# A three-stage kernel on one core: the fade of the sub-chunk attention moves from the values to the queries

## Chip, core and metric

The kernel runs on one core of a Trainium2 chip. The metric is the device time of one execution in microseconds (us); the median of several executions counts. TensorE multiplies matrices, VectorE, ScalarE and GpSimd work on elements, and the DMA queues of SyncE (SP) and ScalarE move data between HBM and the on-chip memories SBUF and PSUM.

## What is computed

Three stages run one after the other: a retention attention over 4 x 8 heads of 768 positions with 64 values each, and two MLPs over the 3072 tokens (512 to 2048 to 512), one with x cos(x), one with a quadratic ramp. The change touches the attention only.

```python
def _attn_ref(q, k, v):
    B, H, S, D = q.shape
    gamma = 1.0 - 2.0 ** (-5.0 - np.arange(H, dtype=np.float32))
    scale = 1.0 / np.sqrt(D)
    state = np.zeros((B, H, D, D), dtype=np.float32)
    for t in range(S):
        state = gamma[None, :, None, None] * state + np.einsum('bhd,bhe->bhde', k[:, :, t], v[:, :, t])
        y[:, :, t] = scale * np.einsum('bhd,bhde->bhe', q[:, :, t], state)
```

The power of gamma that a query at position t carries is called its fade here; the powers that the keys carry are their decay.

## The kernel before

**Order.** The instruction order of every engine is written out by hand. The work is a list of steps. Step i issues the first product of the first MLP for one block of 512 tokens and 128 hidden features (`first`, L681, 12 matmuls), the activation of it (`act`), and the second product of the step three before it (`second`, L768, 12 matmuls). The attention, which makes the blocks of tokens, and the conversion of weights are woven into the first 40 steps. Step 5 begins at 62.2 us in the trace, step 10 at 90.4, step 11 at 95.8, step 12 at 102.4, step 13 at 111.6, step 16 at 137.4.

**The attention.** There are 24 chunks n: six places in the sequence of 128 positions, for each of four batches. Chunks 0 to 7 work on whole chunks, chunks 8 to 23 (n >= NEW) on sub-chunks of 64. For those, `scores64` (L487 for the scores, L498 for the new state) runs on TensorE in step 11, 12, 13, 14 for chunks 8 to 11 and in every second step from 16 for the rest. `masks64` on VectorE then multiplies the scores by the table `mtab` into the tile m (L523, two instructions) and adds the state into w (L536, two or four). One step later `attend` multiplies w by m on TensorE (L580). The tile m holds queries in the two halves where row block and half agree, and masked scores in the other two. `finish_high` multiplies the result by the table `dtab` on VectorE (L614), ScalarE copies the high part (L139), and `finish_low` subtracts it on VectorE (L622). `decay_k` multiplies the keys by a table on GpSimd (L448); `decay_q` does the same to the queries of chunks 4 to 7 alone (L458). In a step of n >= NEW the scores of chunks 8 to 11 stand behind `second`, those of the later chunks ahead of it.

**The conversions.** Weights come as 64-bit numbers and are converted in a chain of steps: a load to `raw` on SP (L189), two VectorE instructions one step later (L203, L206), a third with its ScalarE partner and a GpSimd add (L221, L213, L230), and in the third step a ScalarE copy and GpSimd subtraction (L139, L142) for weights that stay, or a store on ScalarE's queue (L239). A new conversion begins in steps 5 to 11, 16 to 27, and then in odd steps and from step 34.

**The tables.** `mtab` and `dtab` have one buffer each. `load_dtab` is issued on SP in steps 8, 16, 24 and 32 for the next place in the sequence. SP's queue works in order, so a load that waits for its buffer holds those behind it.

Of the kernel before, what the change touches and what calls it, by code (L numbers as in the profile page):

```python
# [17 lines left out]
ALU = mybir.AluOpType  # L18
# [22 lines left out]
def tile_retention_mlp_mlp(  # L41
# [16 lines left out]
    nc = tc.nc  # L58
    NCH = qk.shape[0]
    T, DM = out.shape  # L60
    NF = w1.shape[0]
    NH = NF // 2
    NP = DM // P
    NC = kdec.shape[1]
    NB = T // TB
    D = 64
    CB = TB // C
    NEW = 2 * CB
# [49 lines left out]
    def duo(x, y):  # L118
        if min(x, y) < 6:
            return bank(x), bank(y)  # L120
        t = both()
        return t[:, x - 6, :], t[:, y - 6, :]

    def single(x):
        return bank(x) if x < 6 else both()[:, x - 6, :]
# [12 lines left out]
    def high_part(hi, x):  # L138
        nc.scalar.activation(out=hi, in_=x, func=AF.Copy)  # L139
# [200 lines left out]
    class Attention:  # L340
# [111 lines left out]
            )  # L452

        def decay_q(self, n):
            if n >= NEW:
                return
            self.qd[n] = self.ring("kq", 3 * TB // 2, 2)[:, :TB].rearrange("p (c t) -> p c t", c=NP)
            nc.gpsimd.tensor_tensor(out=self.qd[n], in0=self.t[n][:, 0], in1=self.qdec, op=ALU.mult)  # L458
# [149 lines left out]
        def finish_high(self, n):  # L608
            j, o = divmod(n, CB)
            if o == 0:  # L610
                xt[0, j] = [xpool.tile([P, NP, TB], F32R, tag=t, name=t) for t in ("xh", "xl")]
            if n >= NEW:
                y = self.y[n]
                nc.vector.tensor_tensor(  # L614
                    out=y, in0=y, in1=self.dtab.rearrange("p (c t) -> p c t", c=NP), op=ALU.mult
                )
            high_part(xt[0, j][0][:, :, o * C:(o + 1) * C], self.y[n])

        def finish_low(self, n):
# [25 lines left out]
    def send_x():  # L645
        for d, t in pieces[:2]:
            nc.scalar.dma_start(out=d, in_=t)
        del pieces[:2]
# [23 lines left out]
    def first(k, b, j, hbank):  # L672
        (wh, wl), (xh, xl) = wt[0, j, 0], xt[k, b]
        h = bank(hbank)
        terms = [(c, w, x) for c in range(NP) for w, x in ((wh, xh), (wl, xh))]
        terms += [(c, wh, xl) for c in range(NP)]
        if (k, b, j) == (0, 0, 1):

            terms.sort(key=lambda t: t[1] is wl)
        for i, (c, w, x) in enumerate(terms):  # L680
            nc.tensor.matmul(  # L681
                out=h, lhsT=w[:, c * P:(c + 1) * P], rhs=x[:, c, :],
                start=(i == 0), stop=(i == len(terms) - 1),
            )
        hs[k, b, j] = h

    def act(k, b, j, done=(), fill=(), mid=(), end=()):


        done = iter(done)  # L690
        now = Parts(k, b, j)
        now.rounded()
        last = parts.pop() if parts else None
        if last:
            last.high()
        now.fraction()
        if last:
            last.low()
        evacuate(done, 2)
        for f in mid:  # L700
            f()
        now.cosine()
        evacuate(done, 2)
        for f in fill:
            f()
        conv.advance()
        for f in end:
            f()
        parts.append(now)
# [592 lines left out]
    def run():  # L1302
        i = 0
        with ExitStack() as es:
            att = Attention(es)
# [6 lines left out]
            todo = [Convert(0, j, a, True) for _, _, j, a in order]  # L1312
# [5 lines left out]
            y = dict(enumerate([c for c in todo[:10] if c.a == 1], 1))  # L1318
            x = dict(enumerate(x))
            todo = todo[10:]  # L1320
# [140 lines left out]
            for n in range(CB, NCH):  # L1461
                c = n % CB
                if n < 3 * CB:
                    i = 11 * (n // CB - 1) + c
# [3 lines left out]
                else:  # L1468
                    i = NH * (n // CB - 1) + 2 * c
# [7 lines left out]
            place = {1: (2, 3), 2: (1, 0)}  # L1477
            for i in range(NH * (NB - 1)):
                load_t, load_kq, load_v, decay, early, late, attend = plan[i]
                now = 5 <= i < 12 if i < 2 * NH else (i < 3 * NH + 4 or i % 2 or i > 33) and bool(todo)  # L1480
                conv.start(todo.pop(0) if now else None, stage)
                first(*steps[i], 4 + i % 2)
                for n in load_t:
                    att.load_t(n)
                    att.load_w(n)
                for n in load_kq:
                    att.load_kq(n)
                for n in load_v:
                    att.load_v(n)
                    att.load_k(n)  # L1490
                if i % NH == NH - 1:
                    att.load_mtab((i + 9) // NH)
                elif i % NH == 0 and i:
                    att.load_dtab((i + 8) // NH)
                for n in decay if i >= LAG else ():
                    att.decay_q(n)
                    att.decay_k(n)
                mid, end, fill = [], [], []
                for n in attend:
                    by, bk = place.get(i, (7, 6))  # L1500
                    yb, kb = duo(by, bk)
                    att.attend(n, yb)
                    att.kv(n, kb)
                    mid += [lambda n=n: att.finish(n), lambda n=n: att.update(n)]
                for n in early:
                    att.scores(n, (6, 7))
                    mid.append(lambda n=n: att.masks(n))
                done = second(i - LAG) if i >= LAG else ()
                for m, b in (((0, 0),), ((1, 0),), ((2, 2), (3, 3)))[i] if i < LAG else ():
                    att.kv(m, single(b))  # L1510
                for n in late:
                    att.scores(n, (6, 7))
                    end.append(lambda n=n: att.masks(n))
                if i < LAG:
                    opening(i, CB + i - 1)
                    for c in {0: [x[2]], 1: [y[2]], 2: [y[3], y[4]]}[i]:
                        c.load(stage)
                    if i < 2:
                        att.load_t(CB + 2 + i)
                else:  # L1520
                    if i - 1 in y:
                        c = y[i - 1]
                        if i == LAG:
                            mid += [c.one, c.two]
                            fill += [c.three, c.four, c.five, c.six]
                        else:
                            for f in (c.one, c.two, c.three, c.four):
                                f()
                            mid += [c.five, c.six]
                    act(*steps[i], done, fill, mid, end)  # L1530
                    if i == LAG:
                        y[5].load(stage)
                send_x()
                if i in (3, 6):
                    store_parts(i // 6)
                elif i >= 2 * NH and i % NH == 2:
                    store_parts(steps[i][1])
# [7 lines left out]
        with ExitStack() as es:  # L1545
            stage = es.enter_context(tc.tile_pool(name="stage1", bufs=1, reuse_waits="tile"))
            todo = [Convert(*mja, False, True, store=True) for mja in order2[FIRST:READY]]
# [3 lines left out]
            while i < len(steps):  # L1551
# [3 lines left out]
                now = l < NH - 1 if k == 0 else l != NH - 1 and (l != 3 or b > 2) or len(todo) > len(order2) - READY  # L1555
# [5 lines left out]
                n = blocks.index((k, b)) + 1  # L1561
# [40 lines left out]
def _tables(H, S, D):  # L1602

    g = _GAMMA(H).reshape(H // 2, 2)
    scale = 1.0 / math.sqrt(D)
    s, t = np.arange(C)[:, None], np.arange(C)[None, :]
    low = np.where(s <= t, t - s, 0)
    mask = np.where(s <= t, scale, 0.0)[None, None] * g.T[:, :, None, None] ** low
    mask = mask.transpose(2, 0, 1, 3).reshape(C, -1)
    tt = np.arange(C, S)  # L1610
    qd = scale * g[:, :, None] ** (tt - REF)
    qd = qd.reshape(H // 2, 2, -1, C).transpose(2, 1, 0, 3)
    qd = np.repeat(qd, D, axis=1).reshape(-1, 2 * D, H // 2 * C)
    ss = np.arange(S).reshape(-1, C)
    kd = g.reshape(-1)[None, None, :] ** -(ss.T[:, :, None] - REF).astype(np.float64)

    gh = g.T.reshape(2, 2, 2).transpose(0, 2, 1)[::-1]
    tabs = []
    for j in range(2, S // C):
        at = j * C + np.arange(C).reshape(2, D) - REF  # L1620
        grow = gh[:, None, :, :, None, None] ** -at.T[None, :, None, None, :, None].astype(np.float64)
        grow = grow * (np.arange(D)[:, None] <= np.arange(D))[None, :, None, None, None, :]
        fade = scale * g.T[:, :, None, None] ** at.astype(np.float64)
        fade = np.broadcast_to(fade[:, None], (2, D, H // 2, 2, D))
        tabs.append([a.reshape(2 * D, -1) for a in (grow, fade)])
    return [np.ascontiguousarray(a, dtype=np.float32) for a in (mask, qd[0], kd, np.array(tabs))]
# [60 lines left out]
```

## Time and profile before

| | |
|---|---|
| median of 3 runs | 1109.35 us |
| lowest, highest | 1104.76, 1109.6 us |
| profiled execution: its own time | 1102.34 us |
| its span, first to last instruction | 1100.5 us |
| mean granted TensorE clock | 0.996 |
| busy: TensorE | 1071.2 us (97%) |
| busy: VectorE | 802.5 us (73%) |
| busy: GpSimd | 614.9 us (56%) |
| busy: ScalarE | 603.3 us (55%) |

An engine's busy share is a mean over stages with different limits. A view by stretches says where TensorE, the busiest engine, still has idle time; the chain of work that ended last says what it waited for there. A line number names an instruction of the kernel (L614 is line 614); PE is TensorE, DVE is VectorE, ACT is ScalarE, POOL is GpSimd.

### The profile page before, as it was taken

The numbers are of one execution on the slowest core, as the hardware profiler recorded it, in microseconds if no ns is written. First come the engines' busy times: TensorE is split into PE (matmuls) and PEld (weight loads), VectorE is DVE, ScalarE is ACT, GpSimd is POOL, SyncE is SP. The second block draws the span as 40 slices with busy tenths as digits, with TensorE's granted clock in tenths as the row PEclk, the third lists the DMA queues.
The fourth block names the chain that finished last, engine by engine and source line by source line (L and its number), as shares of the span: only waits on it lengthen the run. The fifth ranks groups of instructions, "written<-read, shape, count | busy, mean of one in ns | idle before, by whom it ended". The sixth has DMA issues, their size and how long they took to land.

```text
span 1100.5 us, 17904 instructions
## 1 busy us (share of the span) xinstructions
PE 1071.2 (97%) x6286; PEld 867.0 (79%) x6286; DVE 802.5 (73%) x1101; ACT 603.3 (55%) x1078; POOL 614.9 (56%) x525
## 2 busy tenths in 40 slices
PE   8999999999999999999999899999999999999996
PEld 5677788878888888878887788788888778888884
DVE  5778878887667446859763477777887777978776
ACT  3444334333355445545562666777577676666663
POOL 3734212221246367878995457786559785554642
PEclk9999999999999999999999999999999999999998
DMA  9498389896667589998978576989588899576542
GB/s 341 171 290 277 107 242 308 270 307 186 212 207 267 193 275 324 335 327 283 313 256 284 198 250 224 316 270 385 200 264 288 293 313 366 173 244 205 180 145 86
DMA packets 139896, 279.94 MB, mean 254 GB/s; under 512 B 15520, under 2 KB 41760, under 8 KB 139808
## 3 DMA queue, kind: packets, MB, share of 16 engines
q1 hardware_dynamic: 128000, 257.31, 71.1%
q10 hardware_dynamic: 11808, 21.50, 5.5%
q8 instruction: 50, 0.82, 0.3%
q14 instruction: 38, 0.31, 0.1%
HBM read 195.39 MB, written 83.36 MB: 253 GB/s over the span
## 4 chain that ended last, share of the span: by engine, by line
PE 78%; DMA 9%; DVE 5%; ACT 2%; POOL 2%; issue 2%; SPq 1%; ACTq 0%; DVEq 0%; POOLq 0%
PE b L768 20%; PE b L681 20%; PE b L951 17%; PE y L967 16%; PE b L580 2%; DMA wo<-wp 1%; DMA xTl<-xl 1%; PE b L487 1%; DVE big L1033 1%; DMA qk<-in_qk 1%; DMA xb2t20h<-xhi 1%; DMA xb1t20h<-xhi 1%; PE b L498 1%; DMA wp<-whi 1%; DMA xh<-xTh 1%
## 5 line engine op out<-in xcount | busy, mean ns | idle before, releaser
L719 ACT ACTIVATE r<-b 128x512 int32<-128x512 f32 x96 | 57.1, 595 | 193.1 <-PE b L681 149.9
L724 DVE SCALAR_TENSOR_TENSOR r<-b,r 128x512 f32<-128x512 f32 x96 | 66.1, 688 | 120.1 <-ACT r L719 118.3
L230 POOL TENSOR_TENSOR cf<-cf,cs 128x512 int32<-128x512 int32 x42 | 54.3, 1293 | 145.0 <-DVE cf L221 109.7
L1025 DVE TENSOR_TENSOR xh<-y,xh 128x1024 f32<-128x1024 f32 x88 | 107.0, 1220 | 26.1 <-PE y L967 24.9
L768 PE MATMUL b<-gh,wo 128*128 128x512 f32 x384 | 98.4, 390 | 2.0 <-DVE o L779 1.7
L1103 POOL TENSOR_TENSOR ft<-r,f 128x512 f32<-128x512 f32 x24 | 31.1, 1296 | 121.0 <-PE y L967 91.7
L681 PE MATMUL b<-xh,wi 128*128 128x512 f32 x384 | 95.4, 390 | 0.9 <-DMA xh<-xTh 0.9
L967 PE MATMUL y<-wi,wo 128*128 128x512 f32 x360 | 92.3, 391 | 3.3 <-POOL wi L992 1.8
L951 PE MATMUL b<-wih,wi 128*128 128x512 f32 x320 | 87.4, 390 | 2.8 <-ACT wih L139 2.4
L1025 DVE TENSOR_TENSOR xl<-y,xl 128x1024 f32<-128x1024 f32 x64 | 77.9, 1217 | 12.9 <-PE y L967 12.9
L967 PE MATMUL y<-gh,wo 128*128 128x512 f32 x272 | 85.1, 394 | 2.3 <-DVE xh L1025 2.3
L768 PEld LDWEIGHTS b<-gh,wo 128*128 128x128 f32 x384 | 71.8, 188 | 17.9 <-DVE o L779 2.4
L681 PEld LDWEIGHTS b<-xh,wi 128*128 128x128 f32 x384 | 71.9, 188 | 16.6 <-DMA xh<-xTh 1.8
L967 PEld LDWEIGHTS y<-wi,wo 128*128 128x128 f32 x360 | 67.1, 188 | 19.4 <-POOL wi L992 3.1
L737 ACT ACTIVATE gh<-b 128x512 fp32r<-128x512 f32 x96 | 57.1, 594 | 39.3 <-DVE b L733 39.0
L681 PE MATMUL b<-xh,wih 128*128 128x512 f32 x192 | 75.8, 397 | 2.2 <-ACT wih L139 0.9
L768 PE MATMUL b<-gh,woh 128*128 128x512 f32 x192 | 77.4, 408 | 0.5 <-ACT woh L139 0.5
L681 PE MATMUL b<-xh,wil 128*128 128x512 f32 x192 | 74.4, 390 | 0.0
L768 PE MATMUL b<-gh,wol 128*128 128x512 f32 x192 | 74.0, 391 | 0.0
L951 PEld LDWEIGHTS b<-wih,wi 128*128 128x128 f32 x320 | 59.8, 188 | 16.4 <-ACT wih L139 2.8
L992 POOL TENSOR_TENSOR gl<-ft,gh 128x512 fp32r<-128x512 f32 x56 | 71.8, 1301 | 1.3 <-ACT gh L139 1.3
L733 DVE TENSOR_TENSOR b<-b,r 128x512 f32<-128x512 f32 x96 | 66.6, 694 | 2.5 <-ACT r L730 0.3
(168 smaller groups left out, 2769.7 us busy)
## 6 DMA issues: line engine op xcount, KB each, us to landing
wi<-wp SPq DMA_DIRECT2D x66, 512.0 KB, 4.8
wo<-wp SPq DMA_DIRECT2D x66, 512.0 KB, 5.1
raw<-in_w SPq DMA_DIRECT2D x64, 512.0 KB, 6.1
wp<-whi SPq DMA_DIRECT2D x48, 256.0 KB, 3.2
wp<-s SPq DMA_DIRECT2D x32, 256.0 KB, 3.2
w<-cf ACTq DMA_DIRECT2D x26, 256.0 KB, 5.4
xTh<-xh ACTq DMA_DIRECT2D x24, 256.0 KB, 5.7
xTl<-xl ACTq DMA_DIRECT2D x24, 256.0 KB, 6.2
```

Source lines behind the costliest of these rows:

```text
L230: nc.gpsimd.tensor_tensor(out=f, in0=f, in1=self.s, op=ALU.add)
L681: nc.tensor.matmul(out=h, lhsT=w[:, c * P:(c + 1) * P], rhs=x[:, c, :], start=(i == 0), stop=(i == len(terms) - 1),)
L719: nc.scalar.activation(out=self.r.bitcast(I32), in_=self.h, func=AF.Identity, scale=INV_2PI, bias=0.25)
L724: nc.vector.scalar_tensor_tensor(out=self.r, in0=self.h, scalar=INV_2PI, in1=self.r.bitcast(I32), op0=ALU.mult, op1=ALU.subtract,)
L733: nc.vector.tensor_tensor(out=self.h, in0=self.h, in1=self.r, op=ALU.mult)
L737: nc.scalar.activation(out=self.gh, in_=self.h, func=AF.Copy)
L768: nc.tensor.matmul(out=acc[k, b][e], lhsT=w[:, s], rhs=g, start=(begin and i == 0), stop=(last and i == 2),)
L951: nc.tensor.matmul(out=to, lhsT=w[:, c * P:(c + 1) * P], rhs=x, start=begin and n == 0, stop=n == len(terms) - 1, skip_group_check=not begin,)
L967: nc.tensor.matmul(out=to[:, e, :], lhsT=w[:, e * P:(e + 1) * P], rhs=a, start=begin and m == 0, stop=m == 2, skip_group_check=not begin,)
L992: eng.tensor_tensor(out=lo, in0=self.f.pop((g, q)), in1=hi.bitcast(F32), op=ALU.subtract)
L1025: nc.vector.tensor_tensor(out=a, in0=y, in1=a, op=ALU.add)
L1103: nc.gpsimd.tensor_tensor(out=o, in0=x, in1=z, op=ALU.subtract)
```

## The change

The fade of chunks 8 to 23 is no longer applied to the result of the attention. `decay_q` now multiplies the queries in m by `dtab` on GpSimd, in place, in two instructions per chunk, one for each half of the partitions. That covers the products of the query with the state and the scores of those halves where the query comes from m. The other scores use a query that is loaded apart; their fade is multiplied into the table `mtab` when it is made. `load_dtab` for the next place is issued after the fade of the last chunk of a place, in the step of that fade, and no longer every eight steps. Conversions begin in steps 5 to 10 instead of 5 to 11, and in steps 16 to 28 instead of 16 to 27.

```diff
         def decay_q(self, n):
+            if n >= NCH:
+                return
             if n >= NEW:
+                for r in range(2):
+                    h = slice(r * D, (r + 1) * D)
+                    q = self.m[n][h, r].rearrange("p c u t -> p (c u t)")
+                    nc.gpsimd.tensor_tensor(out=q, in0=q, in1=self.dtab[h], op=ALU.mult)
                 return
...
-            if n >= NEW:
-                y = self.y[n]
-                nc.vector.tensor_tensor(
-                    out=y, in0=y, in1=self.dtab.rearrange("p (c t) -> p c t", c=NP), op=ALU.mult
-                )
             high_part(xt[0, j][0][:, :, o * C:(o + 1) * C], self.y[n])
...
-                now = 5 <= i < 12 if i < 2 * NH else (i < 3 * NH + 4 or i % 2 or i > 33) and bool(todo)
+                now = 5 <= i < 11 if i < 2 * NH else (i < 3 * NH + 5 or i % 2 or i > 33) and bool(todo)
...
-                elif i % NH == 0 and i:
-                    att.load_dtab((i + 8) // NH)
+                elif i == NH:
+                    att.load_dtab(2)
                 for n in decay if i >= LAG else ():
                     att.decay_q(n)
                     att.decay_k(n)
+                    if n > NEW and n % CB == CB - 1:
+                        att.load_dtab(n // CB + 1)
...
+        most = fade.reshape(2, 2, 2, 2, D).transpose(0, 2, 1, 3, 4)
+        most = np.where(np.eye(2)[:, :, None, None, None] > 0, 1.0, most)
+        grow = grow * most[::-1, None]
```

## Rows read from the trace of the kernel before

**Rows 1.** Busy time by stretch: stretch, length, PE, PEld, DVE, ACT, POOL; clock; DMA.

```profile
84.60:102.40 17.80, 17.78 (x137) 14.57 (x137) 14.64 (x21) 9.67 (x18) 10.98 (x9) 1.00 0.91 309
102.40:144.40 42.00, 38.58 (x505) 30.32 (x506) 34.46 (x58) 13.65 (x24) 9.99 (x9) 1.00 0.46 137
144.40:300.00 155.60, 155.60 (x1577) 125.00 (x1577) 120.97 (x215) 59.73 (x105) 34.52 (x29) 1.00 0.83 256
```

**Rows 2.** Chain that ended last, 84 to 146 us: start, length, what.

```profile
101.27 0.62 PE b L487 x32
...
102.36 2.96 PE b L681 x12
105.33 1.08 issue
106.41 1.15 PE b L580 x32
...
114.60 1.46 issue
...
124.25 0.40 issue
```

**Rows 3.** VectorE in order of time, 96 to 113 us: start, length, instruction, idle before.

```profile
96.16 1.15 DVE L203 TENSOR_SCALAR cf<-raw 128x512 f32<-128x512 f32 x1 [1.09 <-DMA raw<-in_w]
...
97.69 0.68 DVE L221 SCALAR_TENSOR_TENSOR cf<-raw,cf 128x512 int32<-128x512 int32 x1
...
99.22 0.69 DVE L724 SCALAR_TENSOR_TENSOR r<-b,r 128x512 f32<-128x512 f32 x1 [0.24 <-ACT r L719]
...
100.43 0.61 DVE L203 TENSOR_SCALAR cf<-raw 128x512 f32<-128x512 f32 x1
...
101.41 1.78 DVE L221 SCALAR_TENSOR_TENSOR cf<-raw,cf 128x512 int32<-128x512 int32 x1
103.11 1.38 DVE L523 TENSOR_TENSOR qk<-b,mtab 64x512 f32<-64x512 f32 x2
104.53 1.78 DVE L536 TENSOR_TENSOR w<-b,w 64x256 f32<-64x256 f32 x4
...
108.31 0.69 DVE L614 TENSOR_TENSOR b<-b,dtab 128x512 f32<-128x512 f32 x1
109.66 0.69 DVE L622 TENSOR_TENSOR xl<-b,xh 128x512 fp32r<-128x512 f32 x1 [0.66 <-ACT xh L139]
...
111.07 1.77 DVE L221 SCALAR_TENSOR_TENSOR cf<-raw,cf 128x512 int32<-128x512 int32 x1
```

**Rows 4.** Lines L458 and L448: duration ns min/median/max, first and last start, forms.

```profile
L458 POOL TENSOR_TENSOR kq<-qk,w x4: 1273/1299/1472, 25.8 to 49.5; 128x512 f32<-128x512 f32 x4
...
L448 POOL TENSOR_TENSOR kd<-kd,kdec_sb x21: 1037/1046/1500, 28.3 to 282.9; 128x512 f32<-128x512 f32 x17, 64x512 f32<-64x512 f32 x4
```

**Rows 5.** Tile dtab, 80 to 110 us: its load on SP, and issue to landing.

```profile
L375 SPq DMA_DIRECT2D dtab<-in_tabs x1: 585/585/585, 89.1 to 89.1; - x1
...
DMA to landing us min/median/max: 4.6/4.6/4.6
```

**Rows 6.** GpSimd in order of time, 92 to 105 us.

```profile
93.80 1.05 POOL L448 TENSOR_TENSOR kd<-kd,kdec_sb 128x512 f32<-128x512 f32 x1
...
101.18 1.46 POOL L142 TENSOR_TENSOR wol<-cf,woh 128x512 fp32r<-128x512 f32 x1 [0.43 <-ACT woh L139]
```

**Rows 7.** GpSimd in order of time, 540 to 546 us.

```profile
543.09 2.91 POOL L142 TENSOR_TENSOR s<-s,whi 128x512 fp32r<-128x512 f32 x2
```

**Rows 8.** VectorE in order of time, 542 to 547 us.

```profile
544.89 1.66 DVE L221 SCALAR_TENSOR_TENSOR f<-raw,f 128x512 int32<-128x512 int32 x1
```

**Rows 9.** VectorE's groups, 144.4 to 300 us: count, busy us, mean ns, idle before.

```profile
L221 DVE SCALAR_TENSOR_TENSOR cf<-raw,cf 128x512 int32<-128x512 int32 x18 | 13.2, 732 | 0.0
```

**Rows 10.** GpSimd in order of time, 200 to 320 us.

```profile
229.82 1.05 POOL L448 TENSOR_TENSOR kd<-kd,kdec_sb 128x512 f32<-128x512 f32 x1
```

**Rows 11.** Chain that ended last, 225 to 240 us.

```profile
235.01 0.62 PE b L487 x32
```

## The prediction, written before the changed kernel ran

> **What bounds the kernel now.** I read three views, in this order: the busy time of each engine by stretch, the chain of work that ended last, and the instructions of VectorE and GpSimd in order of time around the first sub-chunks. The reader should first cut the run where the change acts: steps 10 to 39, which is 84.6 to 300 us. In the last 155.6 us of it TensorE is busy for 155.60 [rows 1]: nothing that VectorE or GpSimd saves there can move the end. All the idle time that the change can reach lies in 102.4 to 144.4 us, 42.00 - 38.58 = 3.42 us [rows 1].
>
> The chain shows what that idle time is. From step 11 on one chunk is scored in each step and attended in the next. After the scores VectorE multiplies by the mask table (L523) and adds the state (L536); only then can TensorE attend (L580). Meanwhile TensorE has just the twelve matmuls of the next product (L681, 2.96 us). Step 12 waits 1.08 us, step 13 waits 1.46, steps 14 and 15 about 0.4 each (the first of the two stands) [rows 2]. The mask work itself is 1.38 + 1.78 us [rows 3], plus gaps, a little more than 2.96: about 0.4 is the floor that stays when VectorE starts L523 at once. Step 12 thus has 0.66 us above the floor and step 13 has 1.06. In step 12 the excess is L221, the last instruction of a weight conversion: it held VectorE from 101.41 for 1.78 us, so L523 began at 103.11 although the scores, begun at 101.27, were done at 102.36. In step 13 it is a row of things ahead of L523: the fade (L614, 0.69), 0.66 of waiting for ScalarE's copy before L622, two conversion instructions, and an L221 of 1.77 [rows 2, 3].
>
> **The fade that goes.** Sixteen L614 of 0.69 us leave VectorE, 11.0 us, and with each the 0.66 us wait of L622 for the copy behind it, because the copy can now start when the product is ready [rows 3]. Four of the sixteen lie in steps 12 to 15, the other twelve in the stretch without TensorE idle, where they are worth 0. In step 13 L221 starts some 2 us earlier (0.69 + 0.66 and the two conversion instructions that leave with the moved conversion), so L523 is ready when the scores are: 1.46 falls to about 0.42, **-1.04 us** (bounds -1.06 and 0). Steps 14 and 15 already start L523 on the scores: 0. What is late next there is the mask chain itself.
>
> **The multiplication that comes.** Each of the 16 chunks gets two GpSimd instructions over 64 partitions and 512 values. The nearest row is the fade of the whole-chunk queries, L458, 128x512, median 1299 ns [rows 4]; fewer partitions don't make it shorter in the rows of L448, whose two forms take the same, so I take 1.30. That is 2.6 us per chunk and 41.6 us in all, on an engine that is off the chain. They stand in front of the key decay (L448) of the same chunk. For chunk 8 the table is issued at 89.1 and lands 4.6 us later, at 93.7 [rows 5]; GpSimd reaches this place at 93.80 [rows 6], so there is no wait for the table, and 96.4 is early for scores at 101.27 [rows 2]. Queued behind on GpSimd are L448, the low part of a weight (L142) and the integer add of a conversion (L230); the weights are wanted one to two steps later, so 2.6 us cost nothing by themselves; if a weight's low part came too late, its product would wait for the rest of the 1.46 of L142 [rows 6].
>
> What they cost is VectorE's time. L221 takes 0.68 when GpSimd is still and 1.78 when L142 starts at 101.18 beside it [rows 3, 6]. Where GpSimd runs instructions back to back (two in 2.91 us), L221 takes 1.66 [rows 7, 8]: one VectorE instruction gets in after each GpSimd instruction. So a conversion instruction that meets GpSimd pays 1.66 - 0.68 = 0.98 us. (VectorE's other instructions here read PSUM and keep their 0.69, as L724 does at 99.22 [rows 3].) Before the masks of chunk 8 come six such instructions, three each in steps 10 and 11, and GpSimd is now nearly solid from 93.8 to 105. In step 10 the last two, clean before (L221 0.68), pay 0.98 each; back come 0.24 of waiting at L724 and about 0.5 of the first one's 1.15, which stood locked already: +1.2. In step 11 L203 (0.61) goes to about 1.0, L206 pays 1.0, and L221, locked already for 1.78, now meets the shorter key decay and gives back 0.5: +0.9. L523 then begins near 105.2 instead of 103.11: **+2.1 us** in step 12. The lower bound is -0.66 (no lock, the floor), the upper +4.5 (three at 0.98 less 0.24 in step 10; three at 1.5, a little under 1.66, instead of the 2.68 from 100.43 to 103.11 in step 11) [rows 3]. I take 2.1 because the rows nearest to it, those of this very stretch, already show a lock wherever GpSimd runs beside one of the six.
>
> The Trainium skill ("SBUF — State Buffer", Who interferes with whom) says that VectorE and GpSimd share one pair of ports as an exclusive lock, held for a whole instruction, for VectorE instructions with two SBUF inputs or in a two-port mode. By that rule every overlap costs what is left of GpSimd's instruction; the trace agrees with 1.78 against 0.68. Six overlaps at half of 1.3 us are 3.9 us, of which some 2.0 are there already; less the 0.24 the sum for step 12 would be +1.7 by the rule, +2.1 by the rows. The same skill ("GPSIMD Engine Reference", Key points) calls VectorE about twice as fast for such work: here 0.69 against 2.6, since two half-height instructions replace one.
>
> **After 144 us.** VectorE is busy for 120.97 of 155.6 us [rows 1]. Off go 12 x 0.69 = 8.3; the moved conversion adds at most 3 x 0.73 = 2.2 [rows 9]: 114.9. GpSimd goes from 34.52 to 34.52 + 12 x 2.6 + 1.3 = 67.0, 43% of the time. The 18 conversions and the moved one have 57 instructions that can be locked [rows 9]; 43% of them at 0.98 are 24 us, which gives 139 of 155.6. VectorE stays under TensorE: 0.
>
> **The moved conversion.** It leaves slot 11 and the run of conversions gets slot 28 instead. With it move its 512 KB load on SP's queue, three VectorE, one or two ScalarE, one GpSimd instruction and the 256 KB store on ScalarE's queue. Its gain in steps 12 and 13 is counted above. At slot 28 its load must wait for a raw buffer, and behind it on SP stand kq, v and kd of chunk 19. The key decay of that chunk ran at 229.82 [rows 10], its scores at 235.01 [rows 11]; with 2.6 of fade in front it would end at 233.5, 1.5 us early. I take 0; if the load holds SP for 3 us, +1.5. The table reloads for later blocks wait on GpSimd's fade of the block's last chunk, with kq, v, kd behind them on SP; the next chunk is two steps off, over 11 us (two products of 2.96 in each), and such a load landed in 4.6, so 0.
>
> **Sum:** +2.1 - 1.04 + 0 + 0 = **+1.06 us**, about 1103.4 for the profiled execution of 1102.34. The median shown is 1109.35, 7.0 above that execution and near the top of its runs (1104.76 to 1109.6); there the sum gives **1110.4 us**.
>
> **Rivals.** (1) *The locks miss step 12.* If dtab lands later or the low parts come earlier, the six instructions fall in gaps: -0.66 - 1.04 = -1.7, **1107.7**. For it: the L221 of step 10 is clean now, with GpSimd's instructions on both sides of it. Against: GpSimd gets 5 us more work in 11 us. Even all of the 3.42 us would leave 1105.9. Chance 0.25. (2) *VectorE becomes the bound after 144 us*, the slower case. The place is the conversion triple of every odd step, which follows GpSimd's add, two fades and key decay by 3 to 4 us. It decides from (155.6 - 114.9) / 0.98 = 42 of 57 locked instructions on; all 57 give 114.9 + 55.9 - 155.6 = +15.2, half way +7.6, **about 1118**. Against: the 43%, and the gaps that VectorE spends waiting for ScalarE. Chance 0.08. (3) *The change does nothing on the path*: the gain of step 13 and the locks cancel, or other instructions fill in: **1109.4**. Chance 0.12. My forecast has 0.55.
>
> **Numbers.** A measurement of this kernel can tell about 0.5%, 5.5 us, from no change; the shown runs alone spread over 4.8. Every case but (2) lies inside that. Faster needs 5.5 us out of a stretch that has 3.42, so only the spread of runs could show it: 0.08. Slower: case (2) and the far end of step 12's lock with the late load, +4.5 - 1.04 + 1.5 = +5.0: 0.10. Same: 0.82. The range goes from the lowest run's side, 1104 (case 1 and the spread), to 1115 (that far end), leaving out case (2).
>
> **What would show it.** Right: L614 gone, 32 new GpSimd instructions of 1.0 to 1.3 us, L523 of chunk 8 later than 103.1 with L203, L206, L221 at 1.0 to 1.7 before it, the wait in step 13 near 0.4, TensorE solid after 146 us, and everything behind step 15 about 1 us later. Wrong: TensorE idle after 146 us in front of the scores (GpSimd late), in front of L580 (VectorE late) or of the product (h banks late); or a time that moves by over 5 us with the stretch up to 300 us unchanged, which would put the cause after it.

## Result and profile of the changed kernel

| | before | after |
|---|---|---|
| median | 1104.92 us (13 runs) | 1111.86 us (13 runs) |
| lowest, highest | 1102.38, 1109.6 | 1106.56, 1115.83 |
| ratio, with its 95% interval | | 1.0054 [1.0039, 1.007] |
| profiled execution: its own time, span | 1102.34, 1100.5 | 1108.27, 1106.5 |
| mean granted clock of the profiled execution | 0.996 | 0.991 |

The ratio is taken over all runs and is not the quotient of the two medians (that is 1.0063). By it the change costs 0.0054 x 1104.9 = 6.0 us, between 4.3 and 7.7. The forecast was +1.06 us, well within 0.5%; measured is just over that bound, with an interval that spans it. The absolute time lies in the predicted range, but by luck of the base: with more runs the median of before came down from 1109.35 to 1104.92.

The attention's lines stand six further down in the changed kernel: L493 and L504 are the scores and the state, L529 and L542 the masks, L586 the attending product. `first` is L682, `second` L769, `finish_low` L623, and L461 is the new multiplication on GpSimd.

The profiled executions differ by 6.0 us of span. Step 12 starts at 102.36 us before and at 105.04 after, so 2.7 of it stands ahead of step 12. Of that 2.5 us were there when step 10 began (92.75 against 90.23), before the first new instruction at 96.92: that is the opening, where nothing has changed. The rest, 0.16 us, is a wait for VectorE at the start of step 12. From step 12 to step 16 it is 35.0 us before (102.36 to 137.38) and 39.2 after (105.04 to 144.24), +4.2. From step 16 to the end it is 963.1 and 962.3. The change therefore acts where the prediction looked, and with four times the price.

The busy time by stretch of the changed kernel, columns as in [rows 1]:

```profile
102.40:146.00 43.60, 38.20 (x495) 30.02 (x494) 31.63 (x52) 13.42 (x24) 24.95 (x20) 0.92 0.37 114
146.00:300.00 154.00, 153.53 (x1601) 123.38 (x1600) 122.64 (x204) 59.65 (x105) 61.40 (x49) 1.00 0.84 264
...
108.00:112.00 4.00, 0.05 (x1) 0.01 (x1) 3.83 (x8) 0.60 (x1) 4.00 (x4) 0.81 0.50 188
112.00:114.00 2.00, 1.98 (x33) 1.88 (x33) 1.97 (x3) 0.60 (x1) 1.85 (x3) 0.50 0.00 0
114.00:116.00 2.00, 2.00 (x5) 1.62 (x6) 1.29 (x2) 1.63 (x3) 1.09 (x2) 0.50 0.18 66
```

The second row is what the prediction wanted of the later chunks: TensorE busy for 153.53 of 154.00 us. The first row holds the surprise, and not in the busy time: the granted clock, 1.00 in this stretch before [rows 1], is 0.92. The rows below it say where. TensorE does nothing from 108 to 112, and then works from 112 to 116 at 0.50, which is the level of 1.2 GHz instead of 2.4.

The chain that ended last, same kernel (start, length, what; "issue" is time in which TensorE stands still and the profile names no cause, and each one shown here stands in front of the attending product, which needs the masks):

```profile
105.04 3.03 PE b L682 x12
108.06 3.95 issue
112.02 1.97 PE b L586 x32
113.99 4.51 PE b L769 x12
...
122.55 0.42 issue
122.97 1.15 PE b L586 x32
124.12 2.94 PE b L769 x12
```

Against [rows 2] the wait of step 12 has gone from 1.08 to 3.95 us (+2.87) and that of step 13 from 1.46 to 0.42 (-1.04). Behind the long wait the same 32 matmuls of L586 take 1.97 instead of 1.15 and the twelve of L769 take 4.51 instead of 2.94, as they do one step later: +0.82 and +1.57. Together 2.87 - 1.04 + 2.39 = +4.2 us, which is the difference between steps 12 and 16.

VectorE in order of time ahead of the masks of chunk 8, to be laid beside [rows 3]:

```profile
100.06 0.92 DVE L203 TENSOR_SCALAR cf<-raw 128x512 f32<-128x512 f32 x1 [2.47 <-DMA raw<-in_w]
101.01 1.41 DVE L206 TENSOR_SCALAR cf<-cf 128x512 int32<-128x512 int32 x1
102.34 0.68 DVE L221 SCALAR_TENSOR_TENSOR cf<-raw,cf 128x512 int32<-128x512 int32 x1
...
104.90 1.01 DVE L203 TENSOR_SCALAR cf<-raw 128x512 f32<-128x512 f32 x1
105.95 1.40 DVE L206 TENSOR_SCALAR cf<-cf 128x512 int32<-128x512 int32 x1
107.27 1.53 DVE L221 SCALAR_TENSOR_TENSOR cf<-raw,cf 128x512 int32<-128x512 int32 x1
108.72 1.38 DVE L529 TENSOR_TENSOR qk<-b,mtab 64x512 f32<-64x512 f32 x2
```

GpSimd beside it:

```profile
96.92 2.65 POOL L461 TENSOR_TENSOR qk<-qk,dtab 64x512 f32<-64x512 f32 x2
99.65 1.05 POOL L448 TENSOR_TENSOR kd<-kd,kdec_sb 128x512 f32<-128x512 f32 x1
100.65 1.48 POOL L142 TENSOR_TENSOR wil<-cf,wih 128x512 fp32r<-128x512 f32 x1
103.10 1.28 POOL L230 TENSOR_TENSOR cf<-cf,cs 128x512 int32<-128x512 int32 x1 [0.96 <-DVE cf L221]
104.34 2.72 POOL L461 TENSOR_TENSOR qk<-qk,dtab 64x512 f32<-64x512 f32 x2
107.14 1.11 POOL L448 TENSOR_TENSOR kd<-kd,kdec_sb 128x512 f32<-128x512 f32 x1
```

The masks start 3.68 us into the step (108.72 - 105.04) instead of 0.75. Five of the six conversion instructions are now longer than when GpSimd is still (L203 0.42, L206 0.43, L221 0.68); before it was three. The three of step 10 take 3.01 us in all (2.26 before), the three of step 11 take 3.94 (2.82 before). From the start of the first L203 to the masks it is 8.66 us instead of 6.95: +1.71. The other 1.2 us is that this first L203 starts 4.98 us ahead of step 12 instead of 6.20, because its load landed later (a wait of 2.47 instead of 1.09).

### The profile page after: what moved, and what is told of

It is laid out like the page before. It is cut to its first block, busy times and chain, and to the rows that moved or that the text cites. A ratio compares the mean times of both kernels' runs of the same rounds, so it can differ in the third digit from the quotient of the medians.

```text
span 1106.5 us, 17923 instructions
## 1 busy us (share of the span) xinstructions
PE 1074.5 (97%) x6286; PEld 870.2 (79%) x6286; DVE 804.6 (73%) x1085; ACT 603.1 (55%) x1078; POOL 657.9 (59%) x557
## 4 chain that ended last, share of the span: by engine, by line
PE 71%; DMA 11%; DVE 7%; POOL 5%; issue 3%; ACT 2%; SPq 1%; ACTq 0%; DVEq 0%; POOLq 0%
PE b L952 18%; PE y L968 18%; PE b L769 15%; PE b L682 14%; DMA raw<-in_w 2%; PE b L586 1%; DMA xTl<-xl 1%; DMA wp<-s 1%; DMA xh<-yp 1%; POOL s L142 1%; DVE big L1034 1%; POOL f L142 1%; POOL s L267 1%; PE b L476 1%; PE b L493 1%
## 5 line engine op out<-in xcount | busy, mean ns | idle before, releaser
L769 PE MATMUL b<-gh,wo 128*128 128x512 f32 x384 | 98.9, 391 | 2.8 <-DVE o L780 2.8
L682 PE MATMUL b<-xh,wi 128*128 128x512 f32 x384 | 95.1, 389 | 0.5 <-DMA xh<-xTh 0.5
L769 PEld LDWEIGHTS b<-gh,wo 128*128 128x128 f32 x384 | 71.5, 188 | 19.4 <-DVE o L780 4.6
L682 PEld LDWEIGHTS b<-xh,wi 128*128 128x128 f32 x384 | 72.0, 188 | 15.8 <-DMA xh<-xTh 0.9
L769 PE MATMUL b<-gh,woh 128*128 128x512 f32 x192 | 78.4, 414 | 0.5 <-ACT woh L139 0.5
L682 PE MATMUL b<-xh,wih 128*128 128x512 f32 x192 | 75.5, 396 | 2.0 <-ACT wih L139 0.9
L769 PE MATMUL b<-gh,wol 128*128 128x512 f32 x192 | 74.8, 395 | 0.0
L682 PE MATMUL b<-xh,wil 128*128 128x512 f32 x192 | 74.4, 390 | 0.0
L745 DVE TENSOR_TENSOR gl<-b,gh 128x512 fp32r<-128x512 f32 x96 | 65.7, 685 | 3.8 <-ACT gh L738 1.4
```

What stands on the lines that cost most here:

```text
L682: nc.tensor.matmul(out=h, lhsT=w[:, c * P:(c + 1) * P], rhs=x[:, c, :], start=(i == 0), stop=(i == len(terms) - 1),)
L745: nc.vector.tensor_tensor(out=self.gl, in0=self.h, in1=self.gh.bitcast(F32), op=ALU.subtract)
L769: nc.tensor.matmul(out=acc[k, b][e], lhsT=w[:, s], rhs=g, start=(begin and i == 0), stop=(last and i == 2),)
```

## Experiments

The theory after the result: GpSimd's new work holds VectorE's conversion instructions ahead of the masks of chunk 8, TensorE then waits almost 4 us in step 12, and this idle time lowers its clock for the work behind it. Rivals: the moved conversion is the cause; the later chunks or the new table are; the wait costs its own length and the clock is of no account.

| kernel | median us | ratio to before [95%] | wait in step 12 | the two products behind it | step 12 to 16 | mean granted clock, all runs |
|---|---|---|---|---|---|---|
| before | 1105.39 | | 1.08 | 1.15, 2.94 | 35.0 | 0.9948 |
| after | 1111.86 | 1.0054 [1.0039, 1.007] | 3.95 | 1.97, 4.51 | 39.2 | 0.9919 |
| e1_conv_only | 1106.33 | 1.0001 [0.9983, 1.0018] | 1.39 | 1.15, 2.97 | 34.2 | 0.9946 |
| e2_fade_only | 1111.33 | 1.0043 [1.0027, 1.0058] | 3.95 | 1.48, 4.17 | 38.4 | 0.9920 |
| e3_fill | 1107.33 | 1.0021 [1.0008, 1.0034] | 3.04, filled | 1.08, 2.96 | 35.7 | 0.9945 |
| e4_fade_early | 1105.45 | 1.0009 [0.9991, 1.0027] | 0.90 | 1.15, 2.94 | 33.7 | 0.9942 |
| e5_short_fade | 1104.55 | 0.9997 [0.9981, 1.0012] | 2.00 | 1.44, 4.19 | 36.3 | 0.9946 |
| e6_first_four | 1111.05 | 1.0048 [1.0025, 1.0072] | 3.79 | 1.90, 3.73 | 38.1 | 0.9926 |
| e7_wait_alone | 1108.70 | 1.0036 [1.002, 1.0053] | 3.78 | 1.15, 4.49 | 38.1 | 0.9939 |
| e8_early_mtab | 1104.24 | 0.9983 [0.9961, 1.0005] | 1.09 | 1.15, 2.95 | 33.9 | 0.9945 |

The times of the fourth to sixth column are those of one profiled execution of each kernel; the median, the ratio and the mean clock are over all its runs (12 or 13; 70 of before beside the experiments). Each ratio is to the runs of before that were taken together with that kernel. Where the trace and the ratio disagree, the ratio decides, since the ten profiled executions also differ behind step 16: from there to the end they take between 962.3 us (changed kernel) and 970.9 (e7, whose edit does nothing there), against 963.1 before.

**The moved conversion alone.** The kernel before, with the start of one conversion moved.

```diff
-                now = 5 <= i < 12 if i < 2 * NH else (i < 3 * NH + 4 or i % 2 or i > 33) and bool(todo)
+                now = 5 <= i < 11 if i < 2 * NH else (i < 3 * NH + 5 or i % 2 or i > 33) and bool(todo)
```

> The kernel before with the moved conversion alone: no fade on GpSimd, the fade of the values stays on VectorE. Lock theory (the loss is GpSimd's fades of chunks 8 and 9 locking the conversion instructions ahead of chunk 8's masks, and then TensorE's clock): step 12 waits about 1.1 us as before, step 13 about 0.4 to 0.8 instead of 1.46, granted clock full there, time 0.4 to 1 us under before (ratio 0.999 to 1.0). Rival, the moved conversion is the loss (its load or store in a full DMA queue, VectorE in steps 29 and 30): ratio 1.003 to 1.006 and TensorE idle behind 200 us.

The chain of this kernel:

```profile
106.77 1.39 issue
108.16 1.15 PE b L580 x32
109.31 2.97 PE b L768 x12
...
116.33 0.41 issue
```

The wait of step 13 goes (0.41), and the time does not move: 1.0001. The conversion is neither the cause of the loss nor a gain that can be measured. It also shows that a wait of 1.39 us leaves the clock where it was: 1.15 and 2.97.

**The fade alone.** The changed kernel with the conversions where they were before.

```diff
-                now = 5 <= i < 11 if i < 2 * NH else (i < 3 * NH + 5 or i % 2 or i > 33) and bool(todo)
+                now = 5 <= i < 12 if i < 2 * NH else (i < 3 * NH + 4 or i % 2 or i > 33) and bool(todo)
```

> The changed kernel with the conversion left where it was (steps 5 to 11 and 16 to 27). Lock theory: step 12 waits 3.5 to 4.5 us and the granted clock falls behind the wait as in the changed kernel; step 13 waits 1 to 2 us, since two conversion instructions and a locked third are back in front of its masks; ratio to before 1.005 to 1.008, not better than the changed kernel. Rival, the moved conversion is the loss: ratio 0.998 to 1.001.

```profile
105.42 3.95 issue
109.37 1.48 PE b L586 x32
110.85 4.17 PE b L769 x12
...
119.07 0.42 issue
```

The loss is the fade's: 1.0043 against 1.0054, the same wait of 3.95, and the clock falls here too. One expectation missed: the wait of step 13 is 0.42 without the moved conversion as well. Once step 12 is three to four microseconds longer, VectorE has caught up before the scores of step 13 are there.

**The wait filled.** The changed kernel; ahead of the attending product of chunk 8, and of this one only, fourteen matmuls of zeros are added into a bank that is in use.

```diff
+                    for _ in range(14 if n == NEW else 0):
+                        nc.tensor.matmul(out=acc[0, 1][0], lhsT=warm[:, :P], rhs=warm, start=False, stop=False)
                     att.attend(n, yb)
```

> The changed kernel with 14 matmuls of zeros (128x512, bf16, added to an open sum, which they leave as it is) in TensorE's queue in step 12 between the first product and the attention of chunk 8, where it waits. Lock theory with the clock as second part: the wait of TensorE in step 12 shrinks to about 1 us, L586 takes 1.15 us and the second product 2.95 instead of 1.97 and 4.51, so step 12 is about 2.4 us shorter; ratio to before 1.002 to 1.004. Rival, the wait alone is the whole cost and the clock fell for another reason: lengths 1.97 and 4.51 stay, ratio 1.005 to 1.006.

```profile
107.49 3.04 PE b L1506 x14
110.53 1.08 PE b L586 x32
111.61 2.96 PE b L769 x12
```

The matmuls take the place of the wait and compute nothing that is kept. L586 and L769 are back at 1.08 and 2.96, and 1.0054 - 1.0021 = 0.33%, 3.6 us, come back (about 1.4 to 5.8 by the two intervals). This separates the two parts: with the clock held, the wait alone is left, +2.3 us [0.9, 3.8]. The profiled execution is not the changed kernel's with the clock alone altered: its masks begin 2.58 us into step 12 (107.12 - 104.54) where there it was 3.68, so the time to fill was, by estimate, nearer 2.9 us than 3.95. The rival by which the clock is of no account falls.

**The first two fades earlier.** The changed kernel with the first table loaded in step 4 and the queries of chunks 8 and 9 faded in steps 7 and 8.

```diff
-                elif i == NH:
+                elif i == LAG + 1:
                     att.load_dtab(2)
+                if i in (NH - 1, NH):
+                    att.decay_q(i + 1)
                 for n in decay if i >= LAG else ():
-                    att.decay_q(n)
+                    if n not in (NEW, NEW + 1):
+                        att.decay_q(n)
```

> The changed kernel with the fades of chunks 8 and 9 issued in steps 7 and 8 instead of 10 and 11, and their table loaded in step 4, so that GpSimd has the same work but not ahead of chunk 8's masks. Lock theory: step 12 waits 0.4 to 1.2 us, the clock stays full, step 13 waits about 0.4; ratio to before 0.998 to 1.001. Rival, the loss is in the steps behind 146 us (GpSimd's fades of chunks 12 to 23) or in the moved conversion: ratio stays at 1.004 to 1.006.

```profile
105.26 0.90 issue
106.16 1.15 PE b L586 x32
107.31 2.94 PE b L769 x12
```

All the instructions of the change are still there, two pairs of them some 20 us earlier (74.25 and 82.69 instead of 96.92 and 104.34, less the 2.7 by which the latter execution is late); the wait is 0.90 and the time is that of before, 1.0009. So the same amount of work costs nothing that can be measured when it stands elsewhere. The masks of chunk 16 wait in this kernel for their table (VectorE in order of time):

```profile
197.61 1.39 DVE L529 TENSOR_TENSOR qk<-b,mtab 64x512 f32<-64x512 f32 x2 [2.75 <-DMA mtab<-in_tabs]
```

and L586 of this chunk waits 1.28 us for them. Before, the same wait of VectorE was 0.89 and did not reach TensorE; in the changed kernel it was 1.35 and left TensorE idle for 0.14 us; in e2 it was 2.23, and TensorE waited 1.18.

**The fade cut short.** Each of the 32 instructions takes 8 of its 512 columns.

```diff
-                    nc.gpsimd.tensor_tensor(out=q, in0=q, in1=self.dtab[h], op=ALU.mult)
+                    nc.gpsimd.tensor_tensor(out=q[:, :8], in0=q[:, :8], in1=self.dtab[h, :8], op=ALU.mult)
```

> The changed kernel with each fade on GpSimd cut to 8 of its 512 columns, so that order, waits and queues are the same and only the length of the 32 instructions falls. It leaves out the fade of the other 504 columns of the queries. Lock theory: in steps 10 and 11 the conversion instructions meet fewer GpSimd instructions, step 12 waits 0.4 to 1.4 us, the clock stays full, step 13 waits 0.4; ratio to before 0.998 to 1.001. Rival, it is the new order (queries wait for GpSimd, table reloads hold SP): step 12 waits 3 us or more, ratio 1.004 to 1.006.

```profile
106.06 2.00 issue
108.06 1.44 PE b L586 x32
109.50 4.19 PE b L769 x12
```

The loss is gone from the median (0.9997), as expected of the amount of GpSimd's time. The profiled execution does not fit as well: its wait is 2.00 where 0.4 to 1.4 was expected, since L206 and L221 (1.15 and 1.77) still met the key decay and L142, and the clock fell even so. It is 1.3 us longer between steps 12 and 16 than before, at the edge of what the runs allow; the mean clock of all its runs is that of before, so this execution was probably not a typical one.

**The fade in four chunks only.** GpSimd fades the queries of chunks 8 to 11; from chunk 12 on VectorE fades the result as before, with the tables to match. The moved conversion stays.

```diff
-            if n >= NCH:
+            if n >= NEW + CB:
                 return
...
+            if n >= NEW + CB:
+                y = self.y[n]
+                nc.vector.tensor_tensor(
+                    out=y, in0=y, in1=self.dtab.rearrange("p (c t) -> p c t", c=NP), op=ALU.mult
+                )
...
-        grow = grow * most[::-1, None]
+        if j == 2:
+            grow = grow * most[::-1, None]
```

> The change for chunks 8 to 11 alone (and the moved conversion); chunks 12 to 23 are faded on VectorE as before. Lock theory: nearly the whole loss is in step 12, so step 12 waits 3 to 4.5 us with the fall of the clock behind it, ratio to before 1.003 to 1.006. Rival, the fades of chunks 12 to 23 cost (VectorE locked behind 146 us, late masks of chunk 16): ratio under 1.002.

```profile
104.86 3.79 issue
108.65 1.90 PE b L586 x32
110.56 3.73 PE b L774 x12
```

The loss is there in full (1.0048) with a quarter of the fades. The twelve later chunks, their lock on VectorE and their table reloads cost nothing that can be seen, and bring nothing; the two intervals together would show a difference from the changed kernel of about 3 us. (In this kernel the two products stand at L687 and L774.)

**A wait with no work on GpSimd.** The kernel before; for chunk 8 the first mask multiplication, whose source is PSUM, is issued five times.

```diff
-            for f in range(2):
+            for f in [0] * (4 if n == NEW else 0) + [0, 1]:
```

> The kernel before with the first mask multiplication of chunk 8 issued five times instead of once (the same values each time), four times 0.6 to 0.69 us of VectorE work that reads PSUM, and nothing more on GpSimd. Clock theory: step 12 waits 1.08 + 2.4 to 2.8 = 3.5 to 3.9 us, and though GpSimd does nothing new the granted clock falls, with L580 at 1.5 to 2.0 and the second product at 4.2 to 4.5 us; ratio to before 1.003 to 1.005. Rival, the clock fell because of GpSimd's work or something else in the changed kernel: L580 1.15 and second product 2.95, ratio 1.001 to 1.003.

Chain and busy time by stretch:

```profile
104.94 3.78 issue
108.71 1.15 PE b L580 x32
109.86 4.49 PE b L768 x12
```

```profile
104.94:108.71 3.77, 0.00 (x0) 0.03 (x1) 3.57 (x8) 0.60 (x1) 0.05 (x1) 1.00 0.19 71
...
109.90:112.00 2.10, 2.10 (x5) 1.71 (x6) 1.44 (x4) 0.74 (x3) 0.00 (x0) 0.50 0.22 77
```

GpSimd is still (0.05 us in the wait), and the clock falls all the same: L768 takes 4.49, from 109.9 on at 0.50. The wait is 2.70 us longer than before, the kernel 0.0036 x 1105.4 = 4.0 us [2.2, 5.9]. It is the idle time of TensorE that does it, whoever makes it. The wait of step 13 is again 0.42, here with the L614 of before still in place.

**The early fade, with the table of chunk 16 ahead of the conversion's load.**

```diff
+                if i % NH == NH - 1:
+                    att.load_mtab((i + 9) // NH)
                 conv.start(todo.pop(0) if now else None, stage)
...
-                if i % NH == NH - 1:
-                    att.load_mtab((i + 9) // NH)
-                elif i == NH:
+                if i == LAG + 1:
                     att.load_dtab(2)
```

> The kernel with the fades of chunks 8 and 9 in steps 7 and 8, and the loads of mtab for later places put ahead of the conversion's load in their step on SP's queue. If the 1.3 us that chunk 16's attention waited in the run with early fades came from the late mtab (issued at 190.64 behind a conversion's load, landed at 197.6), that wait goes, the masks of chunk 16 wait for no transfer, and the gain of about 1.3 us of steps 12 to 15 stays: ratio to before 0.997 to 1.0. If the transfer is late because the DMA engines are full, whatever the order, the wait stays at 1 us or more.

```profile
105.92 1.09 issue
...
146.00:300.00 154.00, 154.00 (x1572) 124.20 (x1571) 123.57 (x202) 60.00 (x106) 62.69 (x50) 1.00 0.84 257
```

Chunk 16 no longer waits: TensorE is busy for all of 146 to 300 us. This kernel is 0.9983 of before, -1.9 us [-4.3, +0.6]. It beats the changed kernel; that it beats before is not shown. From step 12 to 16 it is 1.1 us shorter than before, and that is all the gain that the trace shows. Behind step 16 this execution is 6.3 us longer than that of before (969.4 against 963.1), with a granted clock of 0.97 to 0.98 between 500 and 800 us where before has 1.00; no edit touches that stretch, so one execution can't tell what this kernel is worth.

## Why the prediction was right and wrong

**What bounds the kernel, and where the change can act: right.** What the trace shows of the loss lies in steps 12 to 16, and e6 shows that the twelve later chunks count for nothing that these runs can tell. One reading was off by a step: 84.6 us is where step 9 begins, not step 10; no term rests on it.

**Step 12's lock: right in its mechanism, and near in its size.** The sum had +1.2 for the three instructions of step 10 and +0.9 for those of step 11, +2.1 in all. The three of step 10 took 0.75 longer and those of step 11 took 1.12, with gaps and less of ScalarE's wait +1.71 from L203 to the masks. The Trainium skill's rule, which the prediction weighed ("SBUF — State Buffer", Who interferes with whom: an exclusive lock for a whole instruction), gave +1.7 and was the nearer of the two, though it counted six overlaps and five came. The wait grew by more, 2.87, because the raw load of step 10 landed 1.2 us later. This is not clearly the change's: the first L203 starts 6.8 us ahead of step 12 in e3, which has the fades, and 5.0 in e1, which has none.

**Step 13: right as a number, not as a reason.** The wait fell to 0.42 as forecast. But it does so in e1 with the fade still on VectorE, in e2 without the moved conversion, and in e7 with neither edit. Where step 12 is long, VectorE has caught up by step 13 whatever else is changed; where step 12 stays short, the moved conversion alone is enough (e1). The fade's removal was not needed for this 1.04 us.

**The step that failed: the price of a wait.** The sum counted a microsecond of waiting as a microsecond. All of [rows 1] has a granted clock of 1.00, and the prediction took it as given; no term and no rival let it fall. Behind 3.95 us of idle time it fell to 0.50, and L586 and L769 paid 2.39 us more. The terms as measured are +2.87 - 1.04 + 2.39 = +4.2 where +2.1 - 1.04 = +1.06 was forecast. The missing term is not always as large: in the executions of e2, e5, e6 and e7 it is 1.54 to 1.56 us. The trace of before has such a fall too, outside the stretches of [rows 1]: near 1080 us TensorE waits 2.31 us, and behind that the granted clock of 1083 to 1086 us is 0.57. e3 shows the missing term by taking it away, e7 by making it without the change. The runs as a whole say the same: the mean granted clock is 0.9919 over the 13 runs of the changed kernel and 0.9948 over the 70 of before, 0.0029 x 1105 = 3.2 us (with a standard error of about 0.8, so about 1.5 either way; this mean counts idle time at the low clock too, 0.19 x 4.0 = 0.8 us of it in the profiled wait, and falls in other places, as in the opening).

**After 144 us: right.** 32 instructions of L461 came, at 1312 ns in the mean (forecast 1.30 us). GpSimd's groups of the changed kernel from 84 to 300 us, and VectorE's L221 and L206 from 146 to 300, answering to [rows 9]:

```profile
L461 POOL TENSOR_TENSOR qk<-qk,dtab 64x512 f32<-64x512 f32 x32 | 42.0, 1312 | 1.3
```

```profile
L221 DVE SCALAR_TENSOR_TENSOR cf<-raw,cf 128x512 int32<-128x512 int32 x18 | 14.8, 823 | 0.0
L206 DVE TENSOR_SCALAR cf<-cf 128x512 int32<-128x512 int32 x19 | 14.6, 771 | 0.7
```

The same L206 in the kernel before, 146 to 300 us:

```profile
L206 DVE TENSOR_SCALAR cf<-cf 128x512 int32<-128x512 int32 x18 | 7.7, 428 | 0.6
```

L221's mean rose from 732 to 823 ns, L203's from 423 to 484 and L206's, the second of the three, from 428 to 771; together that is some 9 us of lock where 24 was forecast. VectorE was busy for 122.64 us of 154 (119.46 before). The forecast of 139 of 155.6 was too high: at 0.98 us each, 9 us are about 10 of the 57 instructions, by estimate, and not 43% of them. The conclusion, TensorE stays the bound, held, but for 0.47 us of idle time.

**The moved conversion: right.** Forecast at nothing beyond step 13; e1 measures 1.0001, and e2 and the changed kernel lie within each other's intervals.

**The rivals.** That the locks miss step 12 fell: five of six instructions were held. That VectorE becomes the bound after 144 us fell with 153.53 us of TensorE in 154.00. That nothing happens on the path fell too. What happened was in none of them, though the upper bound of step 12's lock, +4.5, was there as a number.

**What stays open.** The trace accounts for +4.2 us of 6.0 [4.3, 7.7]. The other 1.8 is as large as the half-width of the interval. Nothing in the stretches behind step 16 of the profiled execution holds it, though single executions differ by up to 8.6 us there. Its opening was 2.5 us longer than that of before, but the opening's granted clock differs between kernels that are the same there (0.86 in the first 25 us of the changed kernel, 0.93 in e2 and e8, 1.00 in e4), and whether it leans to one side with the change was not settled.

## What to carry to other kernels

Price a new wait on the bounding engine in two parts: its length, and the slower work behind it if the granted clock falls there (1.5 to 2.4 us in these executions); look in the trace of before for what follows its longest waits, over the whole run and not only where the change acts, since the rows of the stretch itself need not show the second part. Work that moves to an idle engine can still hold up a busy one (L206 took 1.41 us beside GpSimd and 0.43 without), so move it to a place in time where the instructions that it would meet are not ahead of a critical one: some 20 us earlier, the same work cost nothing that could be measured. And where an absolute time is predicted, take the base from enough runs, since here the base moved by 4.4 us and the change by 6.0.

## What the hardware showed that was not expected

In these traces TensorE's products kept their full speed behind waits of 0.90, 1.08, 1.09 and 1.39 us in step 12 and slowed behind waits of 2.00, 3.78, 3.79 and 3.95, with a granted clock of 0.50 in the rows of the changed kernel and of e7. The two products behind such a wait took 1.5 to 2.4 us more, four times out of five 1.54 to 1.56: in e7 L580 still ran at full speed and L768 paid all of it (4.49), in the changed kernel both paid. Fourteen matmuls of zeros in the gap kept the clock at 1.00.

For waits between 2.0 and 2.4 us the length alone does not decide. Near 610 us, which no edit touches, TensorE waits 2.38 us for the same ScalarE copy in the kernel before and in e7. The clock (the number behind the busy times) stayed up in the first and fell in the second; the rows are the stretch behind the wait:

```profile
611.80:614.00 2.20, 1.80 (x7) 1.19 (x8) 1.37 (x3) 1.93 (x4) 2.18 (x2) 1.00 1.02 408
```

```profile
618.40:621.00 2.60, 2.57 (x6) 1.85 (x7) 1.68 (x4) 2.33 (x5) 2.53 (x2) 0.50 1.01 395
```

So e5's 2.00 us is of a length at which an execution may pay or not. Of the waits of 3.78 us and more in step 12 all four paid.

The Trainium skill ("TensorE: Matmul & The Clock Gate", What's actually happening) says that the low clock is the default and that activity lifts it; e3 (1.00 with the gap filled) and e7 (0.50 behind an empty one) agree with that.

The lock also depends on how the instructions fall against each other, not only on how busy GpSimd is. L221 of step 10 was clean (0.68) in the changed kernel, in a gap of 0.96 us that GpSimd itself had because its next add waits for this very L221.
